# Loads that cast to bf16 in the DMA in place of fp32 staging and casts on the engines, with the squares as a step of their own

## The chip, the cores and the metric

The kernel runs on one core of a Trainium2 chip. The metric is the device time in microseconds (us) of that core. The span, which the profile prints, runs from the first to the last instruction; it is 1.8 us shorter than the time of the profiled run (266.3 of 268.11 us before).

The engines are called as in the profile: PE is TensorE, PEld its weight loads, DVE is VectorE, ACT is ScalarE, POOL is GpSimd, SP is SyncE. SP issues the loads before the change, POOL after it, except those of p, which stay as they were.

## The reference

Two attention passes are followed by a two-layer network. Every input and the output are fp32.

```python
B, H, S, D = 8, 8, 576, 64          # n_pack = 32
def sm_attn(qq, kk, vv):            # softmax(q k^T / sqrt(D)) v
    ...
p_packed = sm_attn(p, k, v)         # 32 rows attend to 576
out      = sm_attn(q, p_packed, p_packed)   # 576 rows attend to 32
x = out.transpose(0, 2, 1, 3).reshape(B * S, H * D)   # 4608 tokens x 512
h = x @ w_in                        # 512 -> 2048
r = np.maximum(h, 0.0)
return (r * r) @ w_out              # 2048 -> 512
```

## The kernel before

The kernel handles the eight batches one after another and lets them overlap. For each batch it loads k, v and q, transposes k and q on VectorE, computes the scores and p_packed, folds p_packed into w_in (the product is called `M`), computes the normalised weights `a` of the second attention, and then the hidden layer from `M` and `a`, the relu `r`, its square `gT`, and the output.

The order of the instructions on each engine is not written by hand. A small planner in the kernel file takes steps with an estimated duration for each stage, dependencies, and slots (buffers), and books them greedily by priority at build time. A step that "takes" a slot can't start until an earlier one "gives" it back.

Inputs come as fp32 into staging tiles and are cast on an engine:

```python
def dma_kq(self, name, qd):
    src = {"k": k, "q": q}[name]
    f = stg.tile([P, JT * D], F32, name="kq_f", tag="kq")
    nc.sync.dma_start(f, src[self.b, qd * QH:(qd + 1) * QH].rearrange(
        "h (a j) d -> (h a) (j d)", j=JT))
    getattr(self, name)[qd] = f
...
def cast_v(self, qd, i, n, eng):       # also regroups v: (head, group) -> (group, head)
    ...
    cast(eng, self.v[:, :, h0 * D:(h0 + w) * D].rearrange("p g (h d) -> p h g d", d=D),
         v_f[:, h0:h0 + w, :].rearrange("p h (g d) -> p h g d", d=D))
...
def dma_w_in(fq, cp):
    f = stg.tile([P, 2, WCH], F32, name="w_f", tag="w", bufs=NW)
    nc.sync.dma_start(f, w_in[...].rearrange("(c p) f -> p c f", p=P))
    w_f[fq, cp] = f
def cast_w_in(fq, cp, eng):
    cast(eng, w_in_b[:, 2 * cp:2 * cp + 2, fq * WCH:(fq + 1) * WCH], w_f[fq, cp])
```

The relu of two hidden blocks and their square, with the square inside the step of the second relu, so that the step ends, and the planner goes on with its stream, only behind the square:

```python
if fb % 2 == 0:
    ...
    res.append(Step(f"R.{b}.{fb}", st, deps, [("h", 1), ("r", 1)], [("h", 1, None)]))
else:
    st.append(stage([("DVE", 0.78, lambda fb=fb: f1_sq(T[b], fb, V))]))
    res.append(Step(f"F1.{b}.{fb}", st, deps + [f"R.{b}.{fb - 1}"], [("h", 1)],
                    [("h", 1, None), ("r", 2, f"R.{b}.{fb - 1}")]))
```

Two VectorE instructions: the square, `gT = r * r`, and `n_mul`, `a = e * ls`. The order of the loads and the engines that may cast:

```python
ld = load_steps(0) + w_in_load() + load_steps(1) + w_out_load()
for b in range(2, B):
    ld += load_steps(b) + ([pload(2, B)] if b == 2 else [])
plan.stream(0, ld)
...
for nm in "kvq":
    plan.stream(5, sum([cast_steps(b, nm, (A, V, Q) if b == 0 else (Q,)) for b in range(B)], []))
plan.stream(5.5, w_in_cast((Q, V)) + w_out_cast((Q, V)))     # Q is POOL, V VectorE, A ScalarE
```

The softmax here doesn't subtract the row's maximum and nothing guards it: scores larger than these inputs give would overflow.

## Time and profile before

| | before |
|---|---|
| time, median of 3 runs | 268.91 us (268.34 to 269.14) |
| span | 266.3 us |
| TensorE busy | 238.3 us |
| POOL busy with casts and copies | 78.7 us of 82.7 |
| first hidden-layer matmul | 26.11 us |
| TensorE work done by 45 us | 17.8 of 229.9 us |

The last row is a count from the trace: the matmuls that have run by 45 us, each times the time that one takes in a full stretch (0.2156 us for an output matmul, 0.1225 for one of the hidden layer, and so on).

From the page of the kernel before: the busy times, and the span in 40 slices of 6.7 us, where a digit is a busy share in tenths and PEclk the clock granted to TensorE, also in tenths.

```profile
span 266.3 us, 4891 instructions
PE 238.3 (89%) x1840; PEld 135.6 (51%) x1840; DVE 150.6 (57%) x241; ACT 163.4 (61%) x297; POOL 82.7 (31%) x101
...
PE   0554959899699999999999999999999999999992
...
POOL 5341499339766822072307222400000000000000
PEclk9997799999999999999999999999999999999999
...
GB/s 254 328 360 398 381 386 334 249 283 231 217 392 202 392 154 352 167 39 181 372 100 43 164 261 50 42 0 81 40 41 42 39 42 39 61 47 63 75 71 79
```

One caution on PEclk: it shows full speed where nothing was recorded. Batch 0's score matmuls stand 0.24 us apart until 20.2 us and 0.12 us apart later, so TensorE ran at half rate there.

TensorE is full from the twelfth slice on. What can be won lies in the first eleven slices, where it is not. There the loads run at up to 398 GB/s, and POOL works most in the same stretch, on casts.

The windows view of the same kernel (columns after the window: its length, then busy us of each engine with the number of instructions, the granted clock, the DMA share and GB/s) says it in numbers:

```profile
0.00:45.00 45.00, 25.46 (x234) 14.91 (x234) 31.85 (x60) 26.07 (x47) 24.84 (x39) 0.92 0.98 348
45.00:90.00 45.00, 41.21 (x335) 24.45 (x333) 32.03 (x51) 27.72 (x53) 28.40 (x35) 1.00 0.99 275
90.00:240.00 150.00, 150.00 (x1182) 86.61 (x1181) 86.77 (x131) 105.46 (x191) 29.46 (x29) 1.00 0.40 113
```

TensorE (the first busy figure) loses 19.5 us in the first 45 and 3.8 in the second 45, and nothing from 90 to 240 us. A cast that takes less time after 90 us is worth nothing by itself.

TensorE's waits, from the view of waits (us in total, times, longest):

```profile
PE ps_a L484 <- DVE pT_bd L352: 8.1, 1, 8.1
PE ps_a L484 <- POOL pT_bd L352: 2.5, 1, 2.5
PE ps_s L580 <- DVE pq_bd L352: 2.5, 1, 2.5
...
PE ps_pp L519 <- POOL v_b L352: 1.8, 2, 1.2
```

The first is the start. The second is a wait for POOL at 66 to 68.7 us, and the last is for POOL's cast of v. These waits and the others sum to 22.0 us.

### The profile page before, as it was taken

The page shows a single profiled execution, that of the slowest core. Times are in us where ns is not written, and L with a number is a line of the kernel's source. Part 1 is how long each engine was busy: PE and PEld are TensorE (multiplying, and loading weights), DVE is VectorE, ACT ScalarE, POOL GpSimd, SP SyncE. Part 2 cuts the span into 40 slices and gives each one's busy share as a digit, 9 for nine tenths or more (in the row PEclk, how much of TensorE's full clock was granted, in tenths as well). Part 3 has the DMA queues.
Part 4 walks back from the last instruction along what each step waited for, and adds up shares of the span by engine and source line. Part 5 has one row for each costly group of instructions (what it writes and reads, how often), then busy time and mean ns, then how long its engine had stood idle before and what let it go on. Part 6 is the DMA issues. An engine that isn't in the chain of part 4 may idle for free.

```text
span 266.3 us, 4891 instructions
## 1 busy us (share of the span) xinstructions
PE 238.3 (89%) x1840; PEld 135.6 (51%) x1840; DVE 150.6 (57%) x241; ACT 163.4 (61%) x297; POOL 82.7 (31%) x101
## 2 busy tenths in 40 slices
PE   0554959899699999999999999999999999999992
PEld 0431634465564445765566556645665556554441
DVE  4657869958459695588537964775258332330000
ACT  3546758566384888779657965796478555651110
POOL 5341499339766822072307222400000000000000
PEclk9997799999999999999999999999999999999999
DMA  7999999996999979419931881103111111212223
GB/s 254 328 360 398 381 386 334 249 283 231 217 392 202 392 154 352 167 39 181 372 100 43 164 261 50 42 0 81 40 41 42 39 42 39 61 47 63 75 71 79
DMA packets 26743, 46.97 MB, mean 176 GB/s; under 512 B 5729, under 2 KB 13921, under 8 KB 26721
## 3 DMA queue, kind: packets, MB, share of 16 engines
q1 hardware_dynamic: 26192, 46.55, 57.9%
q8 instruction: 14, 0.23, 0.4%
q10 hardware_dynamic: 528, 0.13, 0.2%
q14 instruction: 9, 0.07, 0.1%
HBM read 37.22 MB, written 9.44 MB: 175 GB/s over the span
## 4 chain that ended last, share of the span: by engine, by line
PE 61%; DMA 22%; SPq 6%; POOL 4%; DVE 3%; ACT 2%; issue 1%; DVEq 0%; POOLq 0%
PE ps_o L644 31%; PE ps_h L618 19%; DMA kq_f<-in_k_dram 6%; DMA out_dram<-o_sb 6%; DMA w_f<-in_moe_w_in_dram 4%; PE ps_a L550 4%; DMA v_f<-in_v_dram 4%; SPq L653 3%; DMA kq_f<-in_q_dram 2%; SPq L407 2%; PE ps_s L580 2%; POOL v_b L352 2%; PE ps_a L484 2%; ACT o_sb L350 2%; DVE a L606 1%
## 5 line engine op out<-in xcount | busy, mean ns | idle before, releaser
L644 PE MATMUL ps_o<-w_out_b,gT 128*128 128x512 bf16 x576 | 143.3, 379 | 0.8 <-DVE gT L635 0.8
L628 ACT ACTIVATE r<-ps_h 128x576 bf16<-128x576 f32 x125 | 76.1, 651 | 45.5 <-PE ps_h L618 44.4
L635 DVE TENSOR_TENSOR gT<-r 128x1152 bf16<-128x1152 bf16 x64 | 54.0, 849 | 53.8 <-ACT r L628 53.5
L644 PEld LDWEIGHTS <-gT 128*128 128x128 bf16 x576 | 54.7, 98 | 53.4 <-issue 4.8
L618 PE MATMUL ps_h<-a,M 128*128 128x288 bf16 x512 | 77.3, 290 | 0.2 <-ACT r L628 0.2
L618 PEld LDWEIGHTS <-M 128*128 128x128 bf16 x512 | 49.8, 99 | 25.5 <-issue 1.5
L350 ACT COPY o_sb<-ps_o 128x512 f32<-128x512 f32 x25 | 14.7, 588 | 24.6 <-DMA out_dram<-o_sb 17.2
L558 ACT ACTIVATE M<-ps_a,rD 128x512 bf16<-128x512 f32 x36 | 24.2, 689 | 8.0 <-PE ps_a L550 7.8
L352 POOL CAST v_b<-v_f 128x1280 bf16<-128x1280 f32 (+1 forms) x16 | 21.3, 1355 | 23.4 <-DMA v_f<-in_v_dram 12.7
L352 POOL CAST q_b<-kq_f 128x1152 bf16<-128x1152 f32 x14 | 17.5, 1259 | 30.9 <-DMA kq_f<-in_q_dram 30.8
L560 DVE TENSOR_SCALAR M<-ps_a,rD 128x512 bf16<-128x512 f32 x28 | 20.8, 747 | 8.2 <-PE ps_a L550 8.0
L467 DVE STREAM_TRANSPOSE qT<-q_b 128x1152 bf16<-128x1152 bf16 x16 | 21.6, 1366 | 4.9 <-POOL q_b L352 4.7
L352 POOL CAST k_b<-kq_f 128x1152 bf16<-128x1152 f32 (+1 forms) x15 | 18.7, 1255 | 8.4 <-DMA kq_f<-in_k_dram 7.7
L484 PE MATMUL ps_a<-pT_bd,kT 128*128 128x128 bf16 x128 | 9.6, 230 | 10.9 <-DVE pT_bd L352 8.1
L550 PE MATMUL ps_a<-w_in_b,pp 64*32 64x512 bf16 x256 | 15.8, 406 | 3.7 <-ACT M L558 1.9
L352 POOL COPY pT_bd<-pT 32x128 bf16<-32x128 bf16 x28 | 10.5, 376 | 17.5 <-PE ps_a L498 16.5
L606 DVE TENSOR_TENSOR a<-e,ls 128x576 bf16<-128x576 bf16 x16 | 15.7, 1007 | 0.0
L484 PEld LDWEIGHTS <-kT 128*128 128x128 bf16 x128 | 8.5, 103 | 12.1 <-DVE kT L473 7.5
L473 DVE STREAM_TRANSPOSE kT<-k_b 128x320 f32<-128x320 f32 (+1 forms) x32 | 14.4, 506 | 0.3 <-POOL k_b L352 0.2
L580 PE MATMUL ps_s<-qT,pq_bd 128*128 128x288 bf16 x64 | 10.8, 305 | 4.1 <-DVE pq_bd L352 2.5
L587 ACT ACTIVATE e<-ps_s,rD 128x576 bf16<-128x576 f32 x16 | 11.3, 739 | 4.3 <-PE ps_s L580 4.3
L550 PEld LDWEIGHTS <-pp 64*32 64x32 bf16 x256 | 4.4, 89 | 17.0 <-issue 15.2
(57 smaller groups left out, 144.9 us busy)
## 6 DMA issues: line engine op xcount, KB each, us to landing
kq_f<-in_k_dram SPq DMA_DIRECT2D x16, 576.0 KB, 7.7
kq_f<-in_q_dram SPq DMA_DIRECT2D x16, 576.0 KB, 8.1
out_dram<-o_sb SPq DMA_DIRECT2D x144, 64.0 KB, 1.7
v_f<-in_v_dram SPq DMA_DIRECT2D x14, 320.0 KB, 5.1
w_f<-in_moe_w_in_dram SPq DMA_DIRECT2D x8, 512.0 KB, 8.6
w_f<-in_moe_w_out_dram SPq DMA_DIRECT2D x8, 512.0 KB, 9.1
v_f<-in_v_dram SPq DMA_DIRECT2D x14, 256.0 KB, 6.8
v_f<-in_v_dram SPq DMA_DIRECT2D x4, 160.0 KB, 5.8
```

Source lines behind the costliest of these rows:

```text
L350: nc.scalar.copy(dst, src)
L352: eng.tensor_copy(dst, src)
L467: nc.vector.transpose(self.qT[:, qd].rearrange("p dh (j a) -> p j dh a", a=32), self.t.qb[qd][:].rearrange("p (j dh dl) -> p j dh dl", dh= ...
L484: nc.tensor.matmul(ps[:, g * P:(g + 1) * P], lhsT=self.kT[:, qd, g * P:(g + 1) * P].bitcast(BF16).rearrange("p (t two) -> p two t", two=2) ...
L550: nc.tensor.matmul(pss[qd][o:o + 32, :], lhsT=self.pp[64 * e:64 * e + 64, qd * P + pr * 64 + 32 * (e ^ qd):][:, :32], rhs=w_in_b[64 * e:64 ...
L558: nc.scalar.activation(dst, self.psm[c][e], ACT.Copy, scale=self.rD[:, e:e + 1])
L560: nc.vector.tensor_scalar_mul(dst, self.psm[c][e], self.rD[:, e:e + 1])
L606: nc.vector.tensor_tensor(out=self.a2[:, qd, n0:n1].rearrange("p (c n) -> p c n", n=HALF), in0=self.e2[qd, hf], in1=self.ls[qd, hf], op=AL ...
L618: nc.tensor.matmul(ps[:, c, :HALF], lhsT=a.M[:, qd, fb * FB:(fb + 1) * FB], rhs=a.a2[:, qd, c * HALF:(c + 1) * HALF], start=(qd == 0), sto ...
L628: nc.scalar.activation(dst, src, ACT.Relu)
L635: eng.tensor_tensor(out=gT[:, fb - 1:fb + 1, o:o + S], in0=r, in1=r, op=ALU.mult)
L644: nc.tensor.matmul(po[t], lhsT=gT[:, fb, n0:n0 + P], rhs=w_out_b[:, fb, :], start=(fb == 0), stop=(fb == NFB - 1))
```

## The change

The intent is to take the casts off the engines. Every load except those of p, which is still staged in fp32 and cast on VectorE, writes bf16 into its tile, so the staging tiles and their slots go, and with them the layout of batches 0 and 1 that was slow to transpose ("SPREAD"). Loads are issued from POOL, before POOL's memsets. v still has to be regrouped, now by a copy from bf16 to bf16. The first two pieces of w_out are loaded ahead of batch 1. The squares become a step, in a stream of their own. One planning round is added (`ROUNDS`), in which the planner works back from its first plan and orders by how late a step may be.

The core of the diff (cuts marked by three dots; the rest is the memsets' place, removed casts, renamed dependencies, and code for wide output tiles that isn't used):

```diff
             def dma_kq(self, name, qd):
                 src = {"k": k, "q": q}[name]
-                f = stg.tile([P, JT * D], F32, name="kq_f", tag="kq")
-                nc.sync.dma_start(f, src[self.b, qd * QH:(qd + 1) * QH].rearrange(
-                    "h (a j) d -> (h a) (j d)", j=JT))
-                getattr(self, name)[qd] = f
...
+                t = getattr(self, name + "b")[qd] = qkv.tile([P, JT * D], BF16, name=name + "_b", tag="kqb")
+                nc.gpsimd.dma_start(t, src[self.b, qd * QH:(qd + 1) * QH].rearrange("h (a j) d -> (h a) (j d)", j=JT))
...
+            def cast_v(self, qd, eng):
+                h0 = qd * QH
+                cast(eng, v_b[:, :, h0 * D:(h0 + QH) * D].rearrange("p g (h d) -> p h g d", d=D),
+                     self.vr[:, h0:h0 + QH, :].rearrange("p h (g d) -> p h g d", d=D))
...
         def dma_w_in(fq, cp):
-            f = stg.tile([P, 2, WCH], F32, name="w_f", tag="w", bufs=NW)
-            nc.sync.dma_start(f, w_in[cp * 2 * P:(cp + 1) * 2 * P, fq * WCH:(fq + 1) * WCH].rearrange(
-                "(c p) f -> p c f", p=P))
-            w_f[fq, cp] = f
...
+            nc.gpsimd.dma_start(w_in_b[:, 2 * cp:2 * cp + 2, fq * WCH:(fq + 1) * WCH],
+                                w_in[cp * 2 * P:(cp + 1) * 2 * P, fq * WCH:(fq + 1) * WCH].rearrange("(c p) f -> p c f", p=P))
...
-        def load_step(name, us, fn, slot, deps=()):
-            return Step(name, [stage([("SP", 0.45, fn)]), stage([("DMA", us, lambda: None)])], deps, slot, (), lag=1.6)
+        def load_step(name, issue, us, fn, slot, deps=()):
+            return Step(name, [stage([("POOL", issue, fn)]), stage([("-", 1.15, lambda: None)]), stage([("DMA", us, lambda: None)])],
+                        deps, slot + [("dl", 1)], [("dl", 2, None)], lag=0.85)
...
+        def sq_steps(b):
+            res = []
+            for fb in range(1, NFB, 2):
+                deps = [f"R.{b}.{fb - 1}", f"R.{b}.{fb}"]
...
+                res.append(Step(f"F1.{b}.{fb}", [stage([("DVE", 0.77, lambda fb=fb: f1_sq(T[b], fb, V))])], deps, (),
+                                [("r", 0, f"R.{b}.{fb - 1}")]))
+            return res
...
-        ROUNDS = 0
+        ROUNDS = 1
...
-        ld = load_steps(0) + w_in_load() + load_steps(1) + w_out_load()
+        ld = load_steps(0) + w_in_load() + w_out_load()[:2] + load_steps(1) + w_out_load()[2:]
...
-        plan.stream(5.5, w_in_cast((Q, V)) + w_out_cast((Q, V)))
...
+        plan.stream(5.8, sum([sq_steps(b) for b in range(B)], []))
```

The slot `dl` has 8 places: the planner keeps at most eight loads in flight. The diff also takes the number of bf16 k and q tiles (`kqb`) from 4 to 8, gives v two landing tiles in place of one, and loads batch 0 in another order: all of v before q, where before the first q came ahead of v.

## The prediction

> **What bounds it now.** After about 90 us, TensorE: the windows view shows it busy 30.0 of 30 us (100 to 160 us), clock 1.00. From the chain of waits, its needed work: an output matmul 0.2156 us x 576 = 124; a group of 4 hidden-layer matmuls 0.49 x 128 = 63; M 16; scores, sums, attention products 27. Sum about 230 of a span of 266.3 us. So 36 us are lost: 8.1 before the first matmul, 4.7 after the last (261.6), the rest mostly before 90 us.
>
> Up to 50 us the loads are the limit: DMA share about 1.0 at 295 to 395 GB/s, and a cast behind every load. The timeline shows batch 0's scores at 8.1 us, its v cast until 13.4, q until 14.9, w_in until 27.1 (POOL 1.04, VectorE 0.69 us a piece), the first hidden-layer matmul at 26.1 us, at clock 0.50 (25 to 30 us). Batch 1's v is cast at 32.5 to 35.8, w_out until about 48. At 45 us I count only 20 us of useful TensorE work done. Later gaps: 2.54 us at 66 to 68.7 (pT_bd on POOL, behind casts), 0.8, 0.5.
>
> **What the change does.** Removes about 70 us of POOL casts, early VectorE and ScalarE casts, and the fp32 staging slots that hold up SP's issues. Bytes read stay 37.2 MB; bytes written to SBUF halve. The slow kT layout of batches 0 and 1 goes (1.2 against 0.84 us planned). It adds 16 bf16 regroupings of v on VectorE (planned 0.5 us, 8 in all, off the limit later). Issues move from SP (0.39 us) to GpSimd (planned 0.56 to 0.72), still under a transfer (0.58 MB at 390 GB/s, 1.5 us).
> The Trainium skill (DMA: Bandwidth & Descriptors, "SWDGE vs HWDGE vs iDMA") says casts in DMA must be issued from GpSimd; first bytes come later than from SP, so the start loses about 1 us (estimate). SBUF — State Buffer, "Who interferes with whom", says VectorE's 2-port copies lock GpSimd out. This trace agrees: a POOL cast of k takes 1.15 us, at worst 1.70. Now that can only delay issues.
>
> **Sum.** First bytes at 2.5 us, then 390 GB/s: batch 0 in at 12.5 us, first w_in pair 15, all of w_in 24, batch 1 at 36, w_out 44. Batch 0's hidden layer runs from about 17 to 26 us (before: 26 to 38). Then TensorE starves until batch 1 is in: 19 us of work done by 37 us; from there it stays full. 37 + 211 + about 4 of small gaps + 4.7 of tail = 257 us of span; with about 2 us between span and time, minus under 2 us from separate squares (relu runs ahead of output matmuls), 258 us. TensorE's work and the tail don't change.
>
> **Time: 258 us, 8 in 10 between 251 and 265.** Faster by over 2%: 0.83; within 2%: 0.12; slower: 0.05.
>
> **What would show it.** First hidden-layer matmul at 16 to 20 us; loads done by about 105 us instead of 155; DMA at 370 to 395 GB/s up to 45 us; POOL busy under 25 us; TensorE gaps under 2 us in 45 to 90 us.
>
> **What would make it wrong.** Casting transfers below 300 GB/s: all stages slip and it may be slower. Issues held up by VectorE's copies or by slots in GpSimd's one order, with pT_bd behind them. A clock that stays low around the starved 26 to 37 us.

## More of the kernel before

The groups of VectorE instructions with two inputs from SBUF (count, busy us and mean ns of one, then the idle time before them):

```profile
L635 DVE TENSOR_TENSOR gT<-r 128x1152 bf16<-128x1152 bf16 x64 | 54.0, 849 | 53.8 <-ACT r L628 53.5
L606 DVE TENSOR_TENSOR a<-e,ls 128x576 bf16<-128x576 bf16 x16 | 15.7, 1007 | 0.0
```

## The result, and the profile after

The kernel after took 258.67 us (median of four runs, 258.2 to 258.81). Before took 268.93 us in the same rounds. A ratio in this text is the mean time of one kernel's fast runs over the mean of the other's fast runs of the same rounds, so it is not quite the ratio of the medians quoted. Here it is 0.962, with a 95% interval of 0.960 to 0.964: faster.

From the page of the kernel after, the same lines:

```profile
span 256.4 us, 4801 instructions
PE 235.0 (92%) x1840; PEld 134.5 (52%) x1840; DVE 149.5 (58%) x263; ACT 157.6 (61%) x278; POOL 59.6 (23%) x120
...
PE   0348999999999999999999999999999999999992
...
POOL 8855464549555002200700000000000000000000
PEclk9999999999999999999999999999999999999999
...
GB/s 113 194 199 205 205 206 208 210 235 211 227 221 228 224 36 45 129 86 13 147 142 61 3 41 45 41 22 51 54 54 31 43 76 47 41 63 96 72 71 69
```

TensorE is full from the fifth slice on instead of the twelfth. The clock no longer dips after the start. POOL looks as busy as before in the early slices, but about 48 us of its 59.6 are DMA issues now, which count as busy on this engine. Its casts and copies went from 78.7 us to 9.7. The GB/s are what was written: bf16, half of the fp32 that was read.

The windows, where the columns are those of before:

```profile
0.00:45.00 45.00, 28.58 (x260) 17.15 (x261) 29.96 (x62) 23.96 (x44) 27.97 (x55) 1.00 1.15 190
45.00:90.00 45.00, 45.00 (x386) 26.32 (x383) 36.48 (x66) 32.97 (x61) 23.43 (x48) 1.00 1.20 222
90.00:240.00 150.00, 150.00 (x1147) 86.01 (x1145) 83.09 (x137) 98.37 (x171) 8.16 (x18) 1.00 0.28 59
```

From 45 to 90 us TensorE is never idle now. After 90 us nothing differs for it: 150.00 of 150 both times. Counting work instead of busy time gives the same place:

| work done by TensorE, us | by 25 | by 37 | by 45 | by 70 | by 90 | by 130 | by 200 |
|---|---|---|---|---|---|---|---|
| before | 4.5 | 11.6 | 17.8 | 38.7 | 58.1 | 98.3 | 168.5 |
| after | 5.1 | 15.6 | 22.8 | 47.8 | 68.1 | 108.4 | 178.7 |
| lead of after | 0.6 | 4.0 | 5.0 | 9.1 | 10.0 | 10.1 | 10.2 |

The whole gain is there at 90 us, half of it by 45. It is kept to the end. The tail after the last matmul is 4.7 us before and 5.0 after. The span is 9.9 us shorter, of which 6.6 us is less idle time of TensorE (28.0 to 21.4) and 3.3 us less busy time.

TensorE's waits after:

```profile
PE ps_a L455 <- DVE kT L444: 7.3, 3, 6.4
PE ps_s L551 <- ACT pq_bd L348: 3.6, 1, 3.6
PE ps_pp L490 <- DVE v_b L350: 3.5, 1, 3.5
PE ps_a L521 <- DVE M L531: 0.9, 1, 0.9
```

The waits for POOL are gone. The first three belong to batch 0, in the first 18.1 us; all waits sum to 16.4 us.

The instructions with two inputs from SBUF:

```profile
L606 DVE TENSOR_TENSOR gT<-r 128x1152 bf16<-128x1152 bf16 x64 | 47.3, 751 | 29.7 <-PE ps_o L619 16.0 <-ACT r L599 13.5
L577 DVE TENSOR_TENSOR a<-e,ls 128x576 bf16<-128x576 bf16 x16 | 11.7, 754 | 1.0 <-ACT ls L571 1.0
```

Neither shape nor type nor count changed, yet the square went from 849 to 751 ns and `n_mul` from 1007 to 754. Before, 31 of these 80 instructions overlapped a POOL cast or copy in the trace. They had a mean of 1084 ns and a longest of 1823, and the 49 others 752 ns and a longest of 760. After, 4 overlap one, and the 76 others, those beside DMA issues among them, have a mean of 751. The page "SBUF — State Buffer" of the Trainium skill, in "Who interferes with whom", says that VectorE and GpSimd share a pair of SBUF ports and that a VectorE instruction with two SBUF inputs contends with a GpSimd instruction that reads SBUF. In "SBUF: two separate sides" it says that the one that started first holds the ports for its whole instruction. The trace of the kernel before agrees: the eight of the 31 that began before POOL's instruction took 718 to 759 ns, and of the 23 that began inside one, 20 took more than 800. It goes the other way too: POOL's casts of k take 1.15 us, and those of 1.67 to 1.70 stand beside a square or an `n_mul`.

### The profile page after: what moved, and what is told of

Read it like the earlier page. It is cut to its first block, busy times and chain, and to the rows that moved or that the text cites. A ratio compares the mean times of both kernels' runs of the same rounds, so it can differ in the third digit from the quotient of the medians.

```text
span 256.4 us, 4801 instructions
## 1 busy us (share of the span) xinstructions
PE 235.0 (92%) x1840; PEld 134.5 (52%) x1840; DVE 149.5 (58%) x263; ACT 157.6 (61%) x278; POOL 59.6 (23%) x120
## 4 chain that ended last, share of the span: by engine, by line
PE 76%; DMA 16%; SPq 2%; POOL 2%; ACT 1%; issue 1%; ACTq 0%; POOLq 0%
PE ps_o L619 42%; PE ps_h L589 22%; DMA k_b<-in_k_dram 6%; DMA w_in_b<-in_moe_w_in_dram 4%; PE ps_a L521 4%; DMA out_dram<-o_sb 3%; DMA w_out_b<-in_moe_w_out_dram 3%; PE ps_s L551 3%; SPq L628 2%; PE ps_a L455 2%; PE ps_pp L490 1%; PE ps_s L563 1%; ACT o_sb L348 1%; POOL w_in_b L418 1%; PE ps_a L469 1%
## 5 line engine op out<-in xcount | busy, mean ns | idle before, releaser
L619 PE MATMUL ps_o<-w_out_b,gT 128*128 128x512 bf16 x576 | 147.2, 379 | 0.6 <-DMA w_out_b<-in_moe_w_out_dram 0.6
L599 ACT ACTIVATE r<-ps_h 128x576 bf16<-128x576 f32 x126 | 79.9, 650 | 22.9 <-PE ps_h L589 17.8
L606 DVE TENSOR_TENSOR gT<-r 128x1152 bf16<-128x1152 bf16 x64 | 47.3, 751 | 29.7 <-PE ps_o L619 16.0
L531 DVE TENSOR_SCALAR M<-ps_a,rD 128x512 bf16<-128x512 f32 x38 | 27.9, 748 | 21.2 <-PE ps_a L521 21.2
L410 POOL DMA_DIRECT2D v_r<-in_v_dram x32 | 18.8, 593 | 20.0 <-DVE gT L606 11.1
L529 ACT ACTIVATE M<-ps_a,rD 128x512 bf16<-128x512 f32 x26 | 17.6, 687 | 7.6 <-PE ps_a L521 7.6
L348 ACT COPY pq_bd<-pp 32x64 bf16<-32x64 bf16 x32 | 7.7, 241 | 12.3 <-DVE pp L350 11.8
L405 POOL DMA_DIRECT2D q_b<-in_q_dram x16 | 8.9, 559 | 24.7 <-DVE qT L438 18.5
L462 ACT ACTIVATE e<-ps_a 128x512 bf16<-128x512 f32 x16 | 9.0, 597 | 7.9 <-PE ps_a L455 7.8
L350 DVE COPY o_sb<-ps_o 128x512 f32<-128x512 f32 x16 | 11.0, 688 | 3.6 <-PE ps_o L619 3.5
L577 DVE TENSOR_TENSOR a<-e,ls 128x576 bf16<-128x576 bf16 x16 | 11.7, 754 | 1.0 <-ACT ls L571 1.0
## 6 DMA issues: line engine op xcount, KB each, us to landing
w_in_b<-in_moe_w_in_dram POOLq DMA_DIRECT2D x8, 256.0 KB, 10.7
p_f<-in_p_dram SPq DMA_DIRECT2D x1, 384.0 KB, 14.5
```

Of the source, the lines that this page charges most:

```text
L348: nc.scalar.copy(dst, src)
L410: nc.gpsimd.dma_start(self.vr[32 * i:32 * i + 32, h0:h1, :n * D], src[:, :, J0[i] * D:(J0[i] + n) * D])
L529: nc.scalar.activation(dst, self.psm[c][e], ACT.Copy, scale=self.rD[:, e:e + 1])
L531: nc.vector.tensor_scalar_mul(dst, self.psm[c][e], self.rD[:, e:e + 1])
L599: nc.scalar.activation(dst, src, ACT.Relu)
L606: eng.tensor_tensor(out=gT[:, fb - 1:fb + 1, o:o + S], in0=r, in1=r, op=ALU.mult)
```

## The experiments

The first look left several causes for the ten microseconds. The casts on POOL may have held up the chain from a load to its use, or, through the shared ports, VectorE. The squares as a step of their own may have given a better order. The clock, at half rate from 25 to 30 us before and not after, may have cost it. The order or the issuing engine of the loads may count. Each run below undoes or does one of these alone. The times are medians of the runs. Before was run again with each group of kernels; its medians there lay between 267.89 and 269.18 us, and its single runs between about 266 and 272; four of these, 271.22 us and up, are labelled slow and left out of the ratios. The kernel after was run in the first group alone, so a difference of about one microsecond from it is no more than what the groups differ by. All kernels gave correct results.

### The squares alone, on the kernel before

```diff
-                    st.append(stage([("DVE", 0.78, lambda fb=fb: f1_sq(T[b], fb, V))]))
-                    res.append(Step(f"F1.{b}.{fb}", st, deps + [f"R.{b}.{fb - 1}"], [("h", 1)], ...))
+        def sq_steps(b): ...            # as in the kernel after
+        plan.stream(5.8, sum([sq_steps(b) for b in range(B)], []))
```

> The kernel before with one part of the change alone: squares are their own step in the planner; all loads and casts as before. Theory L (the ten microseconds come from the loads and casts; my prediction gave the squares under 2 us): 267 to 269 us, and TensorE's useful work at 45 us stays within 1 us of before (17.8 us). Rival S (the planner's new freedom with the squares brings a large part): 262 to 265 us.

It took 273.04 us (272.35 to 276.41), ratio 1.020 (1.011 to 1.029): about 4.6 us slower than before, outside both expectations. What happened stands in VectorE's timeline (start, length, instruction, and in brackets the idle time before it and what ended it):

```profile
92.52 1.38 DVE L467 STREAM_TRANSPOSE qT<-q_b 128x1152 bf16<-128x1152 bf16 x1 [4.81 <-POOL q_b L352]
93.83 3.07 DVE L606 TENSOR_TENSOR a<-e,ls 128x576 bf16<-128x576 bf16 x2
```

and in TensorE's at the same place:

```profile
98.87 0.63 PE L550 MATMUL ps_a<-w_in_b,pp 64*32 64x512 bf16 x7 [5.20 <-DVE M L560]
```

VectorE waited 4.81 us for POOL's cast of q, then needed 3.07 us for two `n_mul` (about 1.5 us alone) beside POOL casts, and TensorE waited 5.20 us for an `M` that stood behind them in VectorE's order. The clock was at half rate after that stall, from 98 to 102 us. Up to there this kernel was ahead: by 93 us it had done 64.7 us of TensorE's work against 61.0 before. From 93 to 103 us it did 2.6 us of work against 10.0, and it never made that up. So in the profiled runs the separate squares brought 3.7 us by themselves, and one stall beside POOL's casts took twice that away. That the other order made these casts come due at a worse place is the likely reason and was not tested.

### The squares merged again, on the kernel after

```diff
+                else:
+                    st.append(stage([("DVE", 0.77, lambda fb=fb: f1_sq(T[b], fb, V))]))
+                    res.append(Step(f"F1.{b}.{fb}", st, deps + [f"R.{b}.{fb - 1}"], [("h", 1)], ...))
-        plan.stream(5.8, sum([sq_steps(b) for b in range(B)], []))
```

> The kernel after with squares merged into the second relu's step again; loads stay cast in the DMA. Theory L: 259 to 260.5 us (under 2 us lost). Rival S: 262 to 266 us, with new TensorE gaps in front of output or hidden-layer matmuls in 45 to 100 us.

It took 261.09 us (260.85 to 261.7), ratio to before 0.973, between the two expectations. So about 7 of the 10 us come without the squares. In this setting the separate squares are worth 2.4 us (261.09 less 258.67). The same edit costs 4.6 us with POOL's casts, after the stall above, and gains 2.4 without them. Also, the clock dipped to 0.52 from 25 to 30 us here, as it did before, which raised the next question.

### The clock

Two runs keep TensorE busy with idle matmuls that fill 70% of each planned gap up to 50 us: one on the kernel before, one on the kernel after with merged squares.

```diff
     def fills(self, gap, t):
-        return 0
+        return int(0.7 * gap / 0.107) if 8.0 < t < 50.0 else 0
```

> The kernel before with idle matmuls (128x256 on zeroes) put into the planned TensorE gaps of 8 to 50 us, to keep the granted clock up; nothing else changed. The trace of before shows the clock at 0.50 from 25 to 30.3 us, in which about 2.5 us of useful work were done. Theory C (part of the gain is that after never falls to the half clock there): 265.5 to 267.5 us, clock 1.00 from 20 us on. Theory L alone (the clock is no part): 268 to 270 us.

> The kernel after with squares merged (run e2, 261.1 us, whose clock fell to 0.50 at 25 to 30 us while after's stayed at 1.00), plus idle matmuls in the planned gaps of 10.5 to 50 us. If the separate squares help only by keeping the clock up: 258 to 259.5 us, as after. If they help by order: 260.5 to 262 us.

Both restored the clock, to a mean of 0.997 and 0.999, and neither gained: 268.28 us against before (ratio 1.002, 0.990 to 1.015), and 261.51 against 261.09. The same window of the kernel before, first as it is and then with idle matmuls:

```profile
25.00:30.00 5.00, 4.45 (x28) 1.96 (x28) 4.59 (x7) 2.60 (x4) 2.85 (x3) 0.50 1.06 380
```

```profile
25.00:30.00 5.00, 4.63 (x45) 2.97 (x44) 4.49 (x7) 3.04 (x5) 2.86 (x3) 1.00 1.05 381
```

From 25 to 30 us, TensorE at clock 1.00 ran 45 matmuls, but 17 of them are idle ones. The other 28 are as many as the kernel before ran at 0.50 (one more for `M`, one fewer for the hidden layer). By 45 us both had run the same useful matmuls, 44 of the hidden layer and 10 of the output among them, 17.8 us of work. The skill's page "TensorE: Matmul & The Clock Gate", in "Part 1: The HAM clock gate", states the half rate after an idle window of about 3.4 us, and the 0.50 and 0.52 agree; these runs show that the half rate was a symptom here. It cost no work even in its own stretch.

### The weights alone

The weights' loads and casts were tried on both sides. First, the kernel before with only w_in and w_out cast in the DMA, issued from POOL, the rest from SP as it was:

```diff
         def dma_w_in(fq, cp):
-            f = stg.tile([P, 2, WCH], F32, name="w_f", tag="w", bufs=NW)
-            nc.sync.dma_start(f, ...)
+            nc.gpsimd.dma_start(w_in_b[...], ...)       # and so for w_out
-        plan.stream(5.5, w_in_cast((Q, V)) + w_out_cast((Q, V)))
```

> The kernel before with only w_in and w_out cast in the DMA from GpSimd (16 casts gone from VectorE and POOL); k, q, v, p and squares as before. Theory L, if the weights' casts are the costly ones: 262 to 265 us, hidden layer of batch 0 starts before 24 us. If it is the k, q, v casts that cost, or the squares (S): 266 to 269 us.

It took 268.08 us, ratio 0.998 (0.990 to 1.006): the same. Then the kernel after with the weights staged in fp32, loaded by SP and cast on POOL or VectorE:

```diff
         def dma_w_in(fq, cp):
-            nc.gpsimd.dma_start(w_in_b[...], ...)
+            f = stg.tile([P, 2, WCH], F32, name="w_f", tag="w", bufs=6)
+            nc.sync.dma_start(f, ...)                   # and so for w_out
+        plan.stream(5.5, w_in_cast((Q, V)) + w_out_cast((Q, V)))
```

> The kernel after with w_in and w_out through fp32 staging from SP and casts on POOL and VectorE, all else as after. Theory L with weights as the main part: 262 to 265 us; weights unimportant: 258.5 to 260.5 us. A cast on POOL also delays the issues behind it, so more than the sum may be lost.

It took 269.04 us, ratio 1.003 (0.997 to 1.008): the whole gain was gone, more than either expectation allowed. Read alone, it would say that the weights' casts are worth all of the ten microseconds, and the run before it that they are worth nothing. Both runs have a flaw in common that their traces show: their loads come from two issuers at once. In the kernel after, the weights are issued behind batch 0 in one queue. With SP issuing the weights, they are served beside batch 0. k landed at 9.9 us instead of 5.5, v at 20.3 instead of 12.3, and TensorE started late:

```profile
10.82 1.03 PE L466 MATMUL ps_a<-pT_bd,kT 128*128 128x128 bf16 x8 [10.82 <-DVE kT L455]
```

The skill's page "DMA: Bandwidth & Descriptors" states, in "Queues, rings and completion order", that each DMA engine takes turns between the queue rows that have work for it, packet by packet. The late landings agree with that. It is also why the first of the two runs says little: there v of batch 0 landed late as well, and TensorE waited 3.94 us for it.

So the staged weights were run once more, issued from POOL in the one queue:

```diff
-            f = stg.tile([P, 2, WCH], F32, name="w_f", tag="w", bufs=6)
-            nc.sync.dma_start(f, ...)
+            f = stg.tile([P, 2, WCH], F32, name="w_f", tag="w", bufs=6)
+            nc.gpsimd.dma_start(f, ...)
```

> As e4 (after, weights staged in fp32 and cast on POOL and VectorE, 269.0 us), but the fp32 loads of the weights are issued from GpSimd too, in the same order as after, so that all loads share one queue. Theory Q (e4 lost because two queues were served together and batch 0 came late: k landed at 10 instead of 5.5 us): 261 to 264 us, first scores at about 6.5 us. Rival (the casts of the weights themselves cost the ten microseconds): 267 to 270 us.

It took 263.63 us (262.63 to 263.76), ratio 0.983 (0.977 to 0.989). The start of TensorE's timeline:

```profile
7.00 1.04 PE L466 MATMUL ps_a<-pT_bd,kT 128*128 128x128 bf16 x8 [7.00 <-DVE kT L455]
```

The kernel after starts its scores at 6.43 us. So the 10.4 us between the staged weights and the kernel after split into 5.4 for the second queue (269.04 less 263.63) and 5.0 for the weights' staging and casts (263.63 less 258.67). On the kernel after, then, about five of the ten microseconds hang on how the weights come. Here 9 of the two-input instructions overlap a POOL cast or copy, with 973 ns in the mean, and lose 2.0 us together.

### POOL's casts put back, without a use

The strongest test of the ports is a kernel that has the change's loads and, as well, POOL's casts with nobody waiting for them. It casts an unused tile 28 times, as often as k and q were cast from batch 1 on:

```diff
+        junk_f = consts.tile([P, JT * D], F32, name="junk_f")
+        junk_b = [consts.tile([P, JT * D], BF16, name=f"junk_b{i}") for i in range(2)]
...
+        plan.stream(5, [Step(f"J.{b}.{nm}.{qd}", [stage([("POOL", 1.2, lambda qd=qd: nc.gpsimd.tensor_copy(junk_b[qd], junk_f))])],
+                             [f"L{nm}.{b}.{qd}"] + ["Z"])
+                        for b in range(1, B) for nm in "kvq" for qd in QDS if nm != "v"]
+                    )
```

> The kernel after plus 28 casts of unused data on POOL (128x1152 fp32 to bf16, two per k and q of batches 1 to 7, where before had them), which nobody waits for. Theory P (POOL's casts cost before a part by slowing VectorE's two-input operations and by delaying what stands behind them on POOL): the square's mean rises from 751 to 800 ns or more, 259.5 to 262 us. If VectorE has the slack: square slower, time within 0.5 us of after (258.5 to 259.2 us).

The planner bunched fourteen of the casts, which nobody had foreseen. Five runs took 273.33 to 274.65 us and are labelled slow, because they are over 1.5% above the sixth, which took 261.03. The profile is of a run of the slow group, so it shows what a POOL cast can do to VectorE, and neither a size nor the cause of the slow group. VectorE's timeline in it, then POOL's:

```profile
85.98 14.02 DVE L610 TENSOR_TENSOR gT<-r 128x1152 bf16<-128x1152 bf16 x1
```

```profile
84.07 15.32 POOL L823 CAST junk_b<-junk_f 128x1152 bf16<-128x1152 f32 x14
```

One square of 0.75 us stood in VectorE for 14.02 us, until POOL's casts, which ran back to back, had ended at 99.4 us. An `M` waited behind it and TensorE waited 12.0 us for that `M`. The clock fell to half rate from about 93 us on. Whether the stall is what makes a run of this kernel slow is not shown: the fast run was not profiled.

A second kernel spreads the casts, one behind each issue of a k or q load from batch 1 on:

```diff
+                def fn():
+                    L[b].dma_kq(nm, qd)
+                    if b > 0:
+                        nc.gpsimd.tensor_copy(junk_b[qd], junk_f)
-                return load_step(f"L{nm}.{b}.{qd}", 0.56, 1.5, lambda: L[b].dma_kq(nm, qd), [("kqb", 1)])
+                return load_step(f"L{nm}.{b}.{qd}", 1.76 if b > 0 else 0.56, 1.5, fn, [("kqb", 1)])
```

> As e10 (28 casts of unused data on POOL), but each cast stands right behind the issue of its k or q load, so that they come one by one as in before, not 14 in a row (in e10's trace one square stood for 14.0 us beside 14 casts in a row). Theory P: squares beside a POOL instruction take about 1.0 us on average (before: 1005 ns beside, 756 alone), none over 3 us, and the time is 259.5 to 262 us, with all executions alike. If paced casts are hidden: within 0.5 us of after (258.2 to 259.2 us).

Four runs took 268.25 to 268.68 us and are labelled slow; the two fast ones took 262.41 and 266.29, ratio to before 0.986 (0.976 to 0.996). By its fast runs, which are only two, the kernel is 3.7 and 7.6 us slower than the kernel after. The expectation that all executions would be alike failed. The profile is of a slow-labelled run. VectorE, then POOL:

```profile
45.20 6.83 DVE L581 TENSOR_TENSOR a<-e,ls 128x576 bf16<-128x576 bf16 x2 [0.40 <-ACT ls L575]
```

```profile
44.89 1.16 POOL L662 CAST junk_b<-junk_f 128x1152 bf16<-128x1152 f32 x1
45.98 0.55 POOL L409 DMA_DIRECT2D q_b<-in_q_dram x1
46.52 1.16 POOL L662 CAST junk_b<-junk_f 128x1152 bf16<-128x1152 f32 x1
...
49.74 1.68 POOL L662 CAST junk_b<-junk_f 128x1152 bf16<-128x1152 f32 x1
```

Even with DMA issues between the casts, two `n_mul` (1.5 us alone) took 6.83 us, one of them 5.2. TensorE waited 4.3 us for `a` in this kernel. In the trace, 16 two-input instructions overlap a cast or copy, and together they are 14.0 us longer than their like; in the bunched kernel 9 of them are 16.4 us longer.

What this shows: in the two traces, POOL casts whose results nobody reads delay VectorE, and through it TensorE; and the three fast runs with such casts are 2.4, 3.7 and 7.6 us slower than the kernel after. What it doesn't show: how much of that is the ports alone, since a cast on POOL also delays the load issues behind it; and why the same kernel has executions as far apart as 261 and 274 us. That the two engines' relative timing decides it in each execution is a guess.

### Order of issue, and the plan

Three small runs on the kernel after ask whether the place of single loads matters, and whether a better plan is to be had.

```diff
+        setup_rest()                    # POOL's memsets ahead of all load issues
-        plan.stream(0.5, [Step("Z", [stage([("POOL", 2.6, setup_rest)])], ["Lq.0.1/1.0"])])
```

> The kernel after with GpSimd's memsets (2.4 us) ahead of the first load issue, as before had them, all else as after. All loads start about 2.5 us later. If the start is bound by the loads all the way to the time when TensorE is full (45 us): 260.5 to 261.5 us. If batch 0's order on VectorE hides it: under 260 us.

```diff
-        ld = load_steps(0) + w_in_load() + w_out_load()[:2] + load_steps(1) + w_out_load()[2:]
+        ld = load_steps(0) + w_in_load() + load_steps(1) + w_out_load()
```

> The kernel after with the first two w_out loads moved behind batch 1's loads (after has them before); all else as after. If output matmuls that fill TensorE while batch 1 is on its way matter: 259.5 to 261 us, with the first output matmul after 36 us instead of 28.6. If batch 1 coming 2.6 us earlier makes up for it: 257.5 to 259 us.

```diff
-                         [stage([("PE", 0.45, lambda qd=qd: T[b].s1(qd))]),
+                         [stage([("PE", 0.45 if b else 0.9, lambda qd=qd: T[b].s1(qd))]),   # and other durations of batch 0
-        SEEDS = ()
+        SEEDS = (1, 8, 51, ...)         # 108 accepted random variations of the plan
```

> The kernel after with the planner's figures for batch 0 set to what after's trace shows (v of batch 0 lands at twice the planned transfer time, TensorE at half speed up to 20 us, first issue at 1.2 us) and with the planner's own random search run over it (108 accepted variations). Same operations, other order. Its planned time falls from 254.3 to 253.1 us and work comes earlier. If order at the start is a part of what is left: 256 to 258 us. If the loads alone bind the start: 258 to 259.5 us.

Memsets first took 259.72 us: the first load is issued 1.8 us later (3.03 us against 1.23) and the end moves by 1.05. "Issued first of all" is thus worth about one microsecond. w_out after batch 1 took 259.6, so the two early pieces are worth about 0.9. The replanned kernel took 259.28 (259.1 to 259.8), 0.6 us slower than the kernel after, although the planner thought its plan better. All three differences are near to what the groups of runs differ by. No version was found that beats the kernel after.

## Why the prediction was right

The time was predicted as 258.0 us and measured as 258.67, inside the range, and the direction is as predicted. Point by point:

- **What bounds it.** Right. TensorE's share after 90 us didn't change (150.00 of 150 in both), the tail hardly changed, and the gain was made before 90 us.
- **Casting transfers keep the rate.** Right, if a little low. The page shows 199 to 210 GB/s written from the third to the eighth slice, which is 400 to 420 GB/s read, worked out by doubling, against 370 to 395 predicted. Batch 1's last q landed at 37.5 us (36 predicted) and w_out's last at 45.2 (44).
- **The start.** Right in direction. The first k landed at 5.5 us instead of 4.3, about 1.2 us later. The first issue itself came at 1.23 us on POOL and at 0.7 on SP. The page "DMA: Bandwidth & Descriptors" of the skill, in "SWDGE vs HWDGE vs iDMA", says that casting transfers must come from GpSimd, which no run here tries to break, and that the other path is faster to set up; the trace agrees: k landed 3.6 us after the first issue on SP and 4.3 after that on POOL.
- **First hidden-layer matmul at 16 to 20 us.** Wrong: 24.73 us, against 26.11 before. Two terms were off. The last q of batch 0 landed at 15.6 us, not at 12.5, and w_in's first pair at 18.6, not at 15. By 15.6 us the POOL queue had written 2.04 MB of bf16, so about 4.1 MB of fp32 was read, and batch 0 is 3.54 MB: about 0.5 MB of w_in had moved beside it. With up to eight loads in flight that is possible; the prediction let each load finish before the next. At 400 GB/s it accounts for 1.3 of the 3.1 us; the rest is open. But the loads weren't what ended last: TensorE began on the first `M` at 20.16 us, 1.5 us after its weights were in. The next point held it.
- **The chain behind the loads of batch 0.** Missed. TensorE had the products for p_packed at 14.5 us, but the planner had put both transposes of q ahead of the extraction on VectorE:

```profile
13.97 1.38 DVE L438 STREAM_TRANSPOSE qT<-q_b 128x1152 bf16<-128x1152 bf16 x1 [0.60 <-DMA q_b<-in_q_dram]
15.59 1.38 DVE L438 STREAM_TRANSPOSE qT<-q_b 128x1152 bf16<-128x1152 bf16 x1 [0.24 <-DMA q_b<-in_q_dram]
16.89 0.39 DVE L350 CAST pp<-ps_pp 128x256 bf16<-128x256 f32 x1
```

  The second transpose waited for q, and the extraction, which doesn't need q, waited behind it. TensorE stood for 3.60 us.
- **19 us of work by 37 us.** Too much: 15.6. On the other side, "about 4 of small gaps" after it was too much as well. From 37 us on 214.3 us of work was left, and 37 plus 214.3 is 251.3 us, where the last matmul ended at 251.4: gaps of 0.1 us. The first error made the time 3.4 us too short and the second 3.9 us too long, so that they cancelled. The number was partly luck; the step that TensorE stays full from there on was right.
- **TensorE gaps under 2 us from 45 to 90 us.** Right: 45.00 busy of 45.
- **Loads done by about 105 us.** Wrong: the last q load landed at 132.9 us (159.3 before). POOL waited 17.0 us for transposes to free a q tile. It cost nothing, because TensorE wasn't waiting.
- **POOL busy under 25 us.** Wrong as written, 59.6. DMA issues count as busy on POOL; without them it is about 12.
- **Squares "under 2 us".** 2.4 us against the same kernel with merged squares. On the kernel before they were 3.7 us ahead until one stall, and ended 4.6 behind.
- **The reason.** Half told. The prediction took the loads, and casts behind each of them, as the limit, and of the shared ports it said that now they "can only delay issues", which sees only POOL's side. Before, VectorE's two-input instructions were 10.3 us longer in sum than their like (31 of them beside POOL casts or copies, 1084 ns against 752), and 5.4 us of that fell before 90 us, where it could matter. How much of it reached TensorE is not shown. Unused casts on POOL alone made the kernel 2.4 to 7.6 us slower in three fast runs. The clock, which the prediction listed as a danger, cost nothing.

How the ten microseconds divide is settled only in part. On the kernel after, undoing the weights' part costs 5.0 us in one queue, undoing the squares 2.4, and the early issue and the early w_out about one each, which is near to what groups of runs differ by. They need not add up, as the squares show by changing sign with the setting. The share of k, q and v with their layout, buffers and order in batch 0, and of the planning round, was not isolated.

## What to carry to other kernels

Look for the stretch in which the bounding engine isn't full, and judge a removed cast by the chain it stood in there, since its share of busy time says little: here 69 us of POOL's casts and copies went, and the kernel gained 10, about 2.4 of it with the squares. Before moving a cast to another engine, list what that engine shares; two-input VectorE instructions that vary from 750 to 1800 ns at one shape are a sign that a POOL instruction stands beside them. When one part of a change is undone, keep the loads in the same queue and the same order, because a second issuer alone moved this kernel by 5.4 us, and do it from both sides, because the same edit cost 4.6 us in one setting and gained 2.4 in the other.

## What the Trainium skill lacked or had wrong

- "SBUF — State Buffer", "Who interferes with whom": it says that the blocked side waits for the whole of the other's instruction. It doesn't say whether the two take turns between instructions. Here they didn't: in the profiled run with bunched casts one square of 0.75 us stood for 14.02 us beside 13 of 14 POOL casts in a row, and with casts spaced by DMA issues an `n_mul` of 0.75 us still took 5.2. Nor did starting first always help: in the latter run two squares that began 0.38 and 0.33 us before a cast, during the DMA issue ahead of it, took 2.16 and 2.10 us.
- "SBUF — State Buffer", "SBUF: two separate sides": its warning that VectorE copies in a two-port mode starve transfers issued from GpSimd showed only faintly here; no run tells whether VectorE's copies ran in that mode. The k, q and v issues took 531 to 665 ns throughout (medians 538, 564 and 590). One w_in issue, beside copies of v, took 880 ns (median 710), and two copies of v beside w_out issues took 644 and 790 ns, where most took 452 to 494. The transfers ran at 199 to 210 GB/s written beside VectorE's copies and casts.
- "DMA: Bandwidth & Descriptors", "Bandwidth": no rate is given for transfers that cast. Here fp32 to bf16 wrote 199 to 210 GB/s, 400 to 420 GB/s read if doubled.
- "DMA: Bandwidth & Descriptors", "Issuing engines are not separate DMA queues": it says that the transfers of several issuers interleave, and that more issuers save only the time of issuing. It doesn't say that they can lose time. Here two issuers cost 5.4 us against one, with the first k landing at 9.9 us instead of 6.1.
- "DMA: Bandwidth & Descriptors", "Latency and other measured facts": it speaks of a fixed cost of about 2 us. With eight loads in flight, issue to landing took a median of 8.5 to 10.7 us, so a plan has to count the loads ahead in the queue.
